# Loads of queries, keys and values moved from just ahead of TensorE's block entries to just behind them

## The chip, the cores and the metric

The kernel runs on one core of one Trainium2 chip. The metric is the device time of one execution in microseconds (us). The kernel before took 391.43 us, the median of three runs (388.89, 391.43 and 392.71 us).

## What is computed

The reference is a retention layer (causal attention with a decay per head in place of a softmax) followed by a mixture of eight experts of which each token uses at most one.

```python
# q, k, v: 8 batches x 8 heads x 576 positions x 64
scores = q @ k.T / sqrt(64)
gamma  = 1 - 2 ** (-5 - head)
x      = (scores * where(i >= j, gamma ** (i - j), 0)) @ v      # as 4608 tokens x 512
# experts: w_gate 512x8, w1 8x512x1024, w2 8x1024x512
for tokens with x @ w_skip > 0:
    e   = argmax(x @ w_gate)
    out = x + softmax(x @ w_gate)[e] * (relu(x @ w1[e]) @ w2[e])
for all others: out = x
```

## The kernel before, in words

**Two stages.** The first stage, to about 148 us, makes the retention output in 36 tiles (`NT`) of 128 rows; nine tiles (`NQ`) cover two batches. The second stage runs the experts over gathered tokens. The change is in the first stage.

**A tile's data.** `u_t[g]` holds the queries and keys of tile g in its first half (s = 0) and the values and the keys in a second layout in its second half (s = 2). Each half is one transfer of 512 KB that SP issues in `load_half` (L513, the transfer L517); the second half of every ninth tile has 256 KB. There are five buffers (`UBUFS`), so a first half can be written only when TensorE has read tile g - 5 for the last time.

**The loop (L857 on).** Step g runs, on TensorE, `scores(g + 1)` (`psc`, `psq`) mixed with `second(g - 1)` (`pxt<-sq,u`), now and then `logits` (`pl`, `pn`), then `state(g)` (`ps_s<-u,kn`) mixed with `values(g - 1)` (`pxt<-u,vs`), then transposes of a finished tile (`px`), and then some of the routing of tokens to experts (`routing`, all on `ps_m`). `in_turn` (L673) mixes two lists of products. GpSimd (POOL) makes `kn` from the second half (`keys(g + 2)`, L602) and `vs` (`rows_of(g + 1)`, L624).

**What sets the order.** TensorE's order is the program's own (a manual schedule). The other queues, SP's among them, are ordered by a scheduler that works from dependences and its own estimate of when an instruction is ready. Second halves are asked for behind the scores of a step, with a wait on TensorE's last product there (L867); first halves at the end of a step, with no wait of their own but that for the buffer (L887); tile 7's first half alone is asked for with the second half (L865, `GLATE = 4`).

**What else SP issues there.** From the time that the first expert is chosen (`choose_first` writes `lead_id`, and SP reads it into a register, L370), SP also loads that expert's weights, 512 KB per transfer (`load_w`, L161), one per step from `weights` (L764).

**The end of the stage.** POOL asks for the first expert's tokens (`xg<-out,gi`, L352) behind the `vs` of the last tiles in its queue, and TensorE turns them (`pt_early`, L741).

A product of plain 32-bit floats is two pairs of instructions on TensorE (a weight load and a matmul each), any other product one pair.

Of the kernel before, what the change touches and what calls it, by code (L numbers as in the profile page):

```python
# [11 lines left out]
F32 = mybir.dt.float32  # L12
# [12 lines left out]
NT = NTOK // P  # L25
# [23 lines left out]
UAHEAD = UBUFS - LAG  # L49
VBUFS = 3  # L50
AHEAD = 5
LEAD = 3
GLATE = 4
GROUPS = (8, 8, 8, 4, 4, 4)
KONE = 2
QD = 32
# [32 lines left out]
def kernel(  # L89
# [9 lines left out]
    nc = tc.nc  # L99
# [15 lines left out]
    def keep_up(n):  # L115
        for _ in range(n):
            nc.tensor.matmul(ps_m, warm[:, :P], warm, start=True, stop=True)
# [375 lines left out]
    with ExitStack() as actx:  # L493
# [19 lines left out]
        def load_half(g, s, after=None):  # L513
            if s == 0:
                u_t[g] = ap.tile([P, 4, NPR, P], F32, tag="u", name=f"u_{g}", bufs=UBUFS)
            n = 1 if s and g % NQ == HALF else 2
            half = nc.sync.dma_start(  # L517
                u_t[g][:, s : s + n].rearrange("p s a i -> p (s a i)"),
                qkv[g, s // 2, :, : n * DM],
            )  # L520
            if after is not None:
                tc.add_manual_dep(
                    half.ins,
                    after.name,
                    mybir.DependencyInfo(mybir.DependencyClass.Sync, mybir.DependencyReason.DATA),
                    reason="the second half begins behind a block of products",
                )

        def last_product():
            return next(i for i in reversed(nc.cur_bb.bb.instructions) if i.engine == mybir.EngineType.PE)  # L530

        nc.scalar.dma_start(tab_sb, tab)
        for g, s in ((0, 0), (1, 0), (0, 2), (2, 0), (1, 2), (3, 0), (2, 2), (3, 2)):
            load_half(g, s)
# [13 lines left out]
        def table(n):  # L548
            times(dq_sb[:, n], mt_sb.unsqueeze(1).broadcast_to([P, NPR, D]), TQ + n, D)
# [11 lines left out]
        def scores(g):  # L561

            u = u_t[g]
            psc_t[g] = [
                pp.tile([P, NPR, P], F32, tag=f"sc{g % 2}", name=f"psc_{g}"),
                pp.tile([P, NPR, D], F32, tag="sc2", name=f"psq_{g}"),
            ]
            for a in range(NPR):
                for c in range(2):
                    q = first(g) if c == 0 else slice(D, P)  # L570
                    for j in range(2):
                        nc.tensor.matmul(  # L572
                            psc_t[g][c][halves[1 - j ^ c], a, : q.stop - q.start],
                            u[halves[j], 1 - j, a, c * D : (c + 1) * D],
                            u[halves[j], j, a, q],
                            start=a == 0,
                            stop=a == NPR - 1,
                            skip_group_check=True,
                        )
                yield  # L580

        def decay(g):

            q = first(g)
            near, far = psc_t.pop(g)
            sc_t[g] = ap.tile([P, NPR, D], F32, tag="sq", name=f"sq_{g}", bufs=2 + LAG)
            nc.vector.tensor_tensor(sc_t[g], far, dq_sb[:, g % NQ // 2], ALU.mult)
            for j in range(2):
                h = halves[1 - j]
                nc.vector.tensor_tensor(  # L590
                    u_t[g][h, j, :, :D], near[h, :, :D], mt_sb[h].unsqueeze(1).broadcast_to([D, NPR, D]), ALU.mult
                )
                if q.stop > D:
                    nc.scalar.copy(u_t[g][h, j, :, D:], near[h, :, D:])  # L594

        def keys(g):
            i = g % NQ
            if i == HALF:
                return
            kn_t[g] = ap.tile([P, NPR, P], F32, tag="kn", name=f"kn_{g}")  # L600
            k = TK + i // 2 * 2
            nc.gpsimd.tensor_tensor(  # L602
                kn_t[g].rearrange("p a (j i) -> p a j i", j=2),
                u_t[g][:, 3].rearrange("p a (j i) -> p a j i", j=2),
                tt_sb[:, k : k + 2, :].rearrange("p j a -> p a j").unsqueeze(3).broadcast_to([P, NPR, 2, D]),
                ALU.mult,
            )
# [10 lines left out]
        def rows_of(g):  # L618

            if 1 < g and g % NQ < 2:  # L620
                clear(g)
            for j in range(2):
                h = halves[1 - j]
                nc.gpsimd.tensor_tensor(  # L624
                    vs_t[g][h, j],
                    u_t[g][h, 2, :, j * D : (j + 1) * D],
                    tt_sb[h, TV + g % NQ // 2, :].unsqueeze(2).broadcast_to([D, NPR, D]),
                    ALU.mult,
                )
# [25 lines left out]
        def second(g):  # L655

            last = g % NQ == HALF
            px_t[g] = pp.tile([P, NPR, P], F32, tag="xt", name=f"pxt_{g}", bufs=2)
            for a in range(NPR):
                for n in range(1 + last):  # L660
                    for j in range(2):
                        h = halves[j]
                        nc.tensor.matmul(  # L663
                            px_t[g][h, a, D:],
                            st_t[g][h, a, :] if n else u_t[g][h, 2, a, j * D : (j + 1) * D],
                            u_t[g][h, j, a, D:] if n else sc_t[g][h, a, :],
                            start=a == 0 and n == 0,
                            stop=False,
                            skip_group_check=True,
                        )  # L670
                yield

        def in_turn(*products):  # L673

            products = list(products)
            while products:
                products = [p for p in products if next(p, p) is not p]

        xt_t = {}

# [20 lines left out]
        def stage_c(g, tag="xn"):  # L701
            b, o = divmod(g, NB)
            px = pp.tile([P, DM], F32, tag=tag, name=f"px_{g}")
            for c in range(NCC):
                nc.tensor.transpose(px[:, c * P : (c + 1) * P], xt_t[b][:, c, o * P : (o + 1) * P], ident)
            xn = ap.tile([P, DM], F32, tag="xn", name=f"xn_{g}")
            nc.scalar.copy(xn.rearrange("t (p c) -> t p c", c=NCC), px.rearrange("t (c p) -> t p c", c=NCC))
            nc.scalar.dma_start(out[g * P : (g + 1) * P, :], xn)
# [92 lines left out]
        def routing(most):  # L801

            for do in added:
                do()
            added.clear()
            for n in range(most):
                if not todo or len(added) == NR or todo[0][1] > g or (n and todo[0][0]):
                    break
                todo.pop(0)[2]()
# [34 lines left out]

        table(0)
        in_turn(scores(0))
        keep_up(NKEEP[0])
        decay(0)
# [8 lines left out]
        for g in range(NT):  # L857
            ahead = g + 1 < NT
            last = g - LAG
            products = [scores(g + 1)] if ahead else []  # L860
            if last >= 0 and last % NQ < HALF:
                products.append(second(last))
            in_turn(*products)
            if g == GLATE:
                load_half(g + UAHEAD - 1, 0, last_product())  # L865
            if g and g + UAHEAD - 1 < NT:
                load_half(g + UAHEAD - 1, 2, last_product())  # L867
            if last >= 0 and last % NQ == HALF:
                in_turn(second(last))
            if ahead:  # L870
                decay(g + 1)
            if g == 0:
                rows_of(1)
            if g + 2 < NT:
                keys(g + 2)
            if g and ahead:
                rows_of(g + 1)
            if g + 1 < len(NKEEP):
                keep_up(NKEEP[g + 1])
            if g < NQ - 1 and g % 2 == 0:  # L880
                table(g // 2 + 1)
            elif g < NQ - 1:
                growth(g // 2 + 1)
            logits(g)
            in_turn(state(g), *([values(last)] if last >= 0 else []))
            if g + 1 != GLATE and g + UAHEAD < NT:
                load_half(g + UAHEAD, 0)  # L887
            if last >= 1:
                stage_c(last - 1)
            routing(0 if g == NT - 1 else 3 if g < starts[KCUT + 1] else 8)  # L890
            weights()
        g = NT
# [521 lines left out]
```

## Time and profile before

| | |
|---|---|
| median of three runs | 391.43 us |
| the profiled execution | 390.34 us |
| its span | 388.6 us |
| TensorE busy | 367.6 us (95%) in 4886 matmuls |
| weight loads of TensorE | 334.5 us (86%) in 4886 |
| VectorE, ScalarE, GpSimd busy | 276.0, 181.7, 152.5 us |
| granted TensorE clock, mean | 0.995 |
| moved by DMA | 106.15 MB, mean 273 GB/s |

The profiled execution is one execution; its time lies 1.09 us below the median of the three runs, and its span leaves out 1.7 us at its ends. Busy times of different engines overlap. The DMA share is the mean busy share of the core's 16 DMA engines.

### The profile page before, as it was taken

The numbers are of one execution on the slowest core, as the hardware profiler recorded it, in microseconds if no ns is written. First come the engines' busy times: TensorE is split into PE (matmuls) and PEld (weight loads), VectorE is DVE, ScalarE is ACT, GpSimd is POOL, SyncE is SP. The second block draws the span as 40 slices with busy tenths as digits, with TensorE's granted clock in tenths as the row PEclk, the third lists the DMA queues.
The fourth block names the chain that finished last, engine by engine and source line by source line (L and its number), as shares of the span: only waits on it lengthen the run. The fifth ranks groups of instructions, "written<-read, shape, count | busy, mean of one in ns | idle before, by whom it ended". The sixth has DMA issues, their size and how long they took to land. (4 is left out here: it accounts for less than half of the span.)

```text
span 388.6 us, 12328 instructions
## 1 busy us (share of the span) xinstructions
PE 367.6 (95%) x4886; PEld 334.5 (86%) x4886; DVE 276.0 (71%) x615; ACT 181.7 (47%) x369; POOL 152.5 (39%) x211
## 2 busy tenths in 40 slices
PE   7899998989999898999999999999999999999991
PEld 3678877777887776888899999999999999999991
DVE  3576677578579794877856767867878768687762
ACT  2464555355544576117445455445545545555311
POOL 5885855555475389260136000420322322002032
PEclk9999999999999999999999999999999999999997
DMA  8989997989999988257899768978899898776511
GB/s 305 404 281 375 394 351 270 347 299 341 320 359 331 313 319 260 63 128 252 261 317 262 264 212 276 327 228 303 275 278 329 249 336 313 233 253 228 142 68 61
DMA packets 49573, 106.15 MB, mean 273 GB/s; under 512 B 6102, under 2 KB 21206, under 8 KB 49511
## 3 DMA queue, kind: packets, MB, share of 16 engines
q1 hardware_dynamic: 40951, 85.81, 65.2%
q0 software_dynamic: 3232, 9.99, 7.9%
q10 hardware_dynamic: 5328, 9.52, 6.5%
q8 instruction: 40, 0.66, 0.7%
q14 instruction: 22, 0.18, 0.1%
HBM read 83.51 MB, written 22.28 MB: 272 GB/s over the span
## 5 line engine op out<-in xcount | busy, mean ns | idle before, releaser
L171 DVE TENSOR_TENSOR wlo_w<-w,whi_w 128x1024 fp32r<-128x1024 f32 x59 | 72.0, 1223 | 37.8 <-ACT whi_w L170 35.4
L170 ACT CAST whi_w<-w 128x1024 fp32r<-128x1024 f32 x59 | 61.7, 1050 | 33.1 <-PE py L465 32.4
L465 PE MATMUL py<-hlo,whi_w 128*128 128x336 f32 (+6 forms) x224 | 67.8, 303 | 0.0
L465 PE MATMUL ph<-xhi,wlo_w 128*128 128x336 f32 (+6 forms) x224 | 67.6, 302 | 0.0
L465 PE MATMUL ph<-xlo,whi_w 128*128 128x336 f32 (+6 forms) x224 | 67.5, 302 | 0.0
L465 PE MATMUL ph<-xhi,whi_w 128*128 128x336 f32 (+6 forms) x224 | 67.5, 301 | 0.0
L465 PE MATMUL py<-hhi,wlo_w 128*128 128x336 f32 (+6 forms) x224 | 67.5, 301 | 0.0
L465 PE MATMUL py<-hhi,whi_w 128*128 128x336 f32 (+6 forms) x224 | 67.4, 301 | 0.0
L1035 POOL DMA_INDIRECT out<-rs,sidx x17 | 21.2, 1245 | 84.0 <-DVE rs L1034 82.8
L624 POOL TENSOR_TENSOR vs<-u,tab_sb 64x256 f32<-64x256 f32 x72 | 46.7, 649 | 9.9 <-DMA u<-qkv 2.7
L602 POOL TENSOR_TENSOR kn<-u,tab_sb 128x512 f32<-128x512 f32 x32 | 33.8, 1057 | 42.5 <-DMA u<-qkv 18.9
L687 PE MATMUL pxt<-u,vs 128*64 128x128 f32 (+1 forms) x576 | 47.8, 269 | 1.6 <-issue 1.6
L473 ACT ACTIVATE hhi<-ph 128x336 fp32r<-128x336 f32 (+8 forms) x61 | 25.8, 423 | 45.3 <-PE ph L465 45.0
L590 DVE TENSOR_TENSOR u<-psc,tab_sb 64x256 f32<-64x256 f32 x72 | 30.3, 420 | 23.4 <-PE pxt L663 7.7
L594 ACT COPY u<-psc 64x256 f32<-64x256 f32 x64 | 23.4, 366 | 48.7 <-DVE u L590 45.6
L465 PEld LDWEIGHTS ph<-xhi,whi_w 128*128 128x128 f32 x224 | 42.3, 189 | 0.1
L465 PEld LDWEIGHTS py<-hlo,whi_w 128*128 128x128 f32 x224 | 42.2, 188 | 0.2 <-DVE hlo L474 0.2
L465 PEld LDWEIGHTS ph<-xlo,whi_w 128*128 128x128 f32 x224 | 42.3, 189 | 0.1
L465 PEld LDWEIGHTS py<-hhi,whi_w 128*128 128x128 f32 x224 | 42.3, 189 | 0.0
L465 PEld LDWEIGHTS ph<-xhi,wlo_w 128*128 128x128 f32 x224 | 42.3, 189 | 0.0
L465 PEld LDWEIGHTS py<-hhi,wlo_w 128*128 128x128 f32 x224 | 42.3, 189 | 0.0
L572 PE MATMUL psc<-u 64*64 64x128 f32 (+1 forms) x576 | 39.1, 272 | 2.3 <-DMA u<-qkv 2.1
(213 smaller groups left out, 780.7 us busy)
## 6 DMA issues: line engine op xcount, KB each, us to landing
u<-qkv SPq DMA_DIRECT2D x68, 512.0 KB, 6.6
w<-w SPq DMA_DIRECT2D x64, 512.0 KB, 5.5
out<-xn ACTq DMA_DIRECT2D x36, 256.0 KB, 5.8
hop<-xg SPq DMA_DIRECT2D x12, 256.0 KB, 5.2
xh<-hop SPq DMA_DIRECT2D x48, 64.0 KB, 4.9
hopy<-yp SPq DMA_DIRECT2D x24, 128.0 KB, 3.4
yr<-hopy SPq DMA_DIRECT2D x6, 512.0 KB
u<-qkv SPq DMA_DIRECT2D x4, 256.0 KB
```

The costliest lines, as they stand in the source:

```text
L170: nc.scalar.copy(hi, t)
L171: nc.vector.tensor_tensor(lo, t, hi.bitcast(F32), ALU.subtract)
L465: nc.tensor.matmul(ps, x, y, start=first and n == 0, stop=last and n == 3 * len(terms) - 1)
L473: nc.scalar.activation(hi, ph, AF.Relu)
L572: nc.tensor.matmul(psc_t[g][c][halves[1 - j ^ c], a, : q.stop - q.start], u[halves[j], 1 - j, a, c * D : (c + 1) * D], u[halves[j], j, a, ...
L590: nc.vector.tensor_tensor(u_t[g][h, j, :, :D], near[h, :, :D], mt_sb[h].unsqueeze(1).broadcast_to([D, NPR, D]), ALU.mult)
L594: nc.scalar.copy(u_t[g][h, j, :, D:], near[h, :, D:])
L602: nc.gpsimd.tensor_tensor(kn_t[g].rearrange("p a (j i) -> p a j i", j=2), u_t[g][:, 3].rearrange("p a (j i) -> p a j i", j=2), tt_sb[:, k ...
L624: nc.gpsimd.tensor_tensor(vs_t[g][h, j], u_t[g][h, 2, :, j * D : (j + 1) * D], tt_sb[h, TV + g % NQ // 2, :].unsqueeze(2).broadcast_to([D, ...
L687: nc.tensor.matmul(pxt[halves[j], a, q], vs_t[g][:, j, a, :], u_t[g][:, j, a, q], start=False, stop=a == NPR - 1, skip_group_check=True,)
L1035: done = nc.gpsimd.indirect_dma_start(out=out, out_offset=bass.IndirectOffsetOnAxis(ap=idx, axis=0), in_=rs[:n], in_offset=None, bounds_ch ...
```

## The change

A function `words` counts the instructions that TensorE has been given so far: four for a product of 32-bit floats, two for any other or a transpose, and one more for every 95. The program takes an entry to a block of 256 to lie where this count is 193 modulo 256. `load_clear` asks, for each half, how far the next entry is: if it is at most 93 words away for a first half, or 68 for a second one, the load is put off until 32 words behind that entry, with a wait on the product that stands there; a load that comes up while another is put off follows it. `load_put_off` issues what is due, and is called in the middle of mixed products as well. The rule holds from step 3 on (`GLATE = 3`); the special case for tile 7 goes away. By the program's own count 14 first halves are put off, by 8 to 121 words (1012 in all), and 9 second halves, by 16 to 135 words (689 in all), ahead of 17 different entries; tile 7's first half is issued 49 words earlier than before.

```diff
--- before.py
+++ after.py
@@ -50,7 +50,12 @@
 VBUFS = 3
 AHEAD = 5
 LEAD = 3
-GLATE = 4
+GLATE = 3
+BLOCK = 256
+ENTRY = 193
+WAITED = 95
+SOON = (93, 68)
+BEHIND = 32
 GROUPS = (8, 8, 8, 4, 4, 4)
 KONE = 2
 QD = 32
@@ -529,6 +534,33 @@
         def last_product():
             return next(i for i in reversed(nc.cur_bb.bb.instructions) if i.engine == mybir.EngineType.PE)
 
+        seen = [0, 0]
+
+        def words():
+
+            traced = nc.cur_bb.bb.instructions
+            for i in traced[seen[0] :]:
+                if i.engine == mybir.EngineType.PE:
+                    seen[1] += 2 if i.is_transpose or i.ins[0].dtype != F32 else 4
+            seen[0] = len(traced)
+            return seen[1] + seen[1] // WAITED
+
+        put_off = []
+
+        def load_clear(t, s):
+
+            n = words()
+            entry = n + (ENTRY - n) % BLOCK
+            soon = g >= GLATE and entry - n <= SOON[s // 2]
+            if put_off or soon:
+                put_off.append((entry + BEHIND if soon else put_off[-1][0], t, s))
+            else:
+                load_half(t, s, last_product() if s else None)
+
+        def load_put_off():
+            while put_off and words() >= put_off[0][0]:
+                load_half(*put_off.pop(0)[1:], last_product())
+
         nc.scalar.dma_start(tab_sb, tab)
         for g, s in ((0, 0), (1, 0), (0, 2), (2, 0), (1, 2), (3, 0), (2, 2), (3, 2)):
             load_half(g, s)
@@ -675,6 +707,7 @@
             products = list(products)
             while products:
                 products = [p for p in products if next(p, p) is not p]
+                load_put_off()
 
         xt_t = {}
 
@@ -861,10 +894,8 @@
             if last >= 0 and last % NQ < HALF:
                 products.append(second(last))
             in_turn(*products)
-            if g == GLATE:
-                load_half(g + UAHEAD - 1, 0, last_product())
             if g and g + UAHEAD - 1 < NT:
-                load_half(g + UAHEAD - 1, 2, last_product())
+                load_clear(g + UAHEAD - 1, 2)
             if last >= 0 and last % NQ == HALF:
                 in_turn(second(last))
             if ahead:
@@ -883,10 +914,11 @@
                 growth(g // 2 + 1)
             logits(g)
             in_turn(state(g), *([values(last)] if last >= 0 else []))
-            if g + 1 != GLATE and g + UAHEAD < NT:
-                load_half(g + UAHEAD, 0)
+            if g + UAHEAD < NT:
+                load_clear(g + UAHEAD, 0)
             if last >= 1:
                 stage_c(last - 1)
+            load_put_off()
             routing(0 if g == NT - 1 else 3 if g < starts[KCUT + 1] else 8)
             weights()
         g = NT
```

No instruction is added on any engine, and the orders of TensorE, VectorE, ScalarE and GpSimd are those of before. SP's queue and its waits change. The first place is SP's queue around tiles 20 to 22 (`u_20` to `u_22`; each tile's first row is its first half, and `PE` in a wait is a product of TensorE). Before:

```order
L517 DMA u_19_1366<-qkv 128x1024 [waits DMAHW1_49,PE_49,DMAHW6_49,Activation_49,Pool_49]
L517 DMA u_19_1366<-qkv 128x1024 [waits DMAHW0_49,PE_49]
L517 DMA u_20_1440<-qkv 128x1024 [waits DMAHW1_49,PE_49,DMAHW4_49,Activation_49,Pool_49]
L517 DMA u_20_1440<-qkv 128x1024 [waits DMAHW3_49,PE_49]
L517 DMA u_21_1508<-qkv 128x1024 [waits DMAHW4_49,PE_49,DMAHW7_49,Activation_49,Pool_49]
L517 DMA u_21_1508<-qkv 128x1024 [waits DMAHW6_49,PE_49]
L517 DMA u_22_1607<-qkv 128x1024 [waits DMAHW2_49,DVE_49,DMAHW7_49,PE_49,Pool_49]
```

With the change:

```order
L522 DMA u_19_1366<-qkv 128x1024 [waits DMAHW0_49,PE_49,DMAHW6_49,Activation_49,Pool_49]
L522 DMA u_19_1366<-qkv 128x1024 [waits DMAHW0_49,PE_49]
L522 DMA u_20_1457<-qkv 128x1024 [waits DMAHW2_49,Activation_49,Pool_49]
L522 DMA u_20_1457<-qkv 128x1024 [waits DMAHW3_49,PE_49]
L522 DMA u_21_1547<-qkv 128x1024 [waits DMAHW5_49,PE_49,DMAHW7_49,Activation_49,Pool_49]
L522 DMA u_21_1547<-qkv 128x1024 [waits DMAHW6_49]
L522 DMA u_22_1607<-qkv 128x1024 [waits DMAHW0_49,DVE_49,DMAHW1_49,PE_49,Pool_49]
```

The first half of tile 20 has lost its wait on TensorE, since it now stands behind the put-off second half of tile 19, whose product is the later one; the second half of tile 21 has lost its own in the same way, behind the put-off first half of that tile.

The second place is SP's queue where the first expert's weights come in (`w_0_0` to `w_0_2`) among the last tiles' halves (`u_33` to `u_35`); `DMAHW3` and the like are the counters on which a transfer's landing is told. Before:

```order
L161 ISA
L161 DMA w_0_0_2522<-w 128x1024 [waits DMAHW2_49]
L517 DMA u_33_2489<-qkv 128x1024 [waits DMAHW3_49,PE_49]
L517 DMA u_34_2602<-qkv 128x1024 [waits DMAHW4_49,PE_49,DMAHW6_49,Activation_49,Pool_49]
L161 ISA
L161 DMA w_0_1_2633<-w 128x1024 [waits DMAHW6_49]
L517 DMA u_34_2602<-qkv 128x1024 [waits DMAHW7_49,PE_49]
L517 DMA u_35_2693<-qkv 128x1024 [waits DMAHW0_49,PE_49,DMAHW1_49,Activation_49,Pool_49]
L161 ISA
L161 DMA w_0_2_2719<-w 128x1024 [waits DMAHW2_49]
L517 DMA u_35_2693<-qkv 128x512 [waits DMAHW3_49,PE_49]
```

With the change:

```order
L166 ISA
L166 DMA w_0_0_2522<-w 128x1024 [waits DMAHW2_49]
L166 ISA
L166 DMA w_0_1_2630<-w 128x1024 [waits DMAHW3_49]
L166 ISA
L166 DMA w_0_2_2717<-w 128x1024 [waits DMAHW4_49]
L522 DMA u_33_2489<-qkv 128x1024 [waits DMAHW6_49,PE_49]
L522 DMA u_34_2642<-qkv 128x1024 [waits DMAHW7_49,Activation_49,Pool_49]
L522 DMA u_34_2642<-qkv 128x1024 [waits DMAHW0_49,PE_49]
L522 DMA u_35_2734<-qkv 128x1024 [waits DMAHW1_49,PE_49,DMAHW2_49,Activation_49,Pool_49]
L522 DMA u_35_2734<-qkv 128x512 [waits DMAHW3_49,PE_49]
```

The second half of tile 33 stood behind one transfer of weights and now stands behind three; the first half of tile 34 stood behind one (with tile 33's half) and now stands behind three as well; tile 35's first half stands behind three and not two, its second half behind the same three as before.

## Rows read from the trace of the kernel before

**Rows 1.** The page, busy us of each engine, share of the span, instructions:

```profile
PE 367.6 (95%) x4886; PEld 334.5 (86%) x4886; DVE 276.0 (71%) x615; ACT 181.7 (47%) x369; POOL 152.5 (39%) x211
```

**Rows 2.** TensorE's waits in 0 to 156 us: us, times, longest:

```profile
PE psc L572 <- DMA u<-qkv: 2.1, 3, 1.2
PE pt_early L741 <- DMA xg<-out,gi: 1.8, 1, 1.8
PE pxt L687 <- issue: 1.6, 2, 1.4
```

**Rows 3.** Timeline of TensorE: start, us, what, [idle before it <- releaser], five places:

```profile
36.93 0.32 PE L572 MATMUL psc<-u 64*64 64x128 f32 x1 [0.25 <-issue]
...
52.81 0.32 PE L687 MATMUL pxt<-u,vs 128*64 128x128 f32 x1 [0.29 <-issue]
...
75.94 0.27 PE L663 MATMUL pxt<-u,sv 64*64 64x64 f32 x1 [0.77 <-issue]
...
82.37 0.33 PE L687 MATMUL pxt<-u,vs 128*64 128x128 f32 x2 [1.35 <-issue]
...
118.56 0.27 PE L572 MATMUL psq<-u 64*64 64x64 f32 x1 [0.45 <-issue]
```

**Rows 4.** Stretches between those places: us, busy (xinstructions) by engine, clock, DMA share:

```profile
52.82:75.95 23.13, 21.08 (x508) 17.11 (x509) 15.88 (x44) 11.15 (x27) 12.42 (x19) 1.00 0.90 311
75.95:82.37 6.42, 5.07 (x127) 4.34 (x127) 5.11 (x16) 2.51 (x7) 3.55 (x6) 1.00 0.97 357
82.37:118.56 36.19, 35.30 (x887) 29.72 (x888) 26.13 (x72) 19.08 (x47) 20.71 (x31) 1.00 0.92 329
```

**Rows 5.** The page, DMA queues: packets, MB, share of 16 engines:

```profile
q8 instruction: 40, 0.66, 0.7%
```

**Rows 6.** Timeline of SP's queue, two loads ahead of the idle at 75.94:

```profile
68.41 0.33 SPq L517 DMA_DIRECT2D u<-qkv  x1
...
70.00 0.33 SPq L517 DMA_DIRECT2D u<-qkv  x1
```

**Rows 7.** The page, DMA issues: KB each, median us from issue to landing:

```profile
u<-qkv SPq DMA_DIRECT2D x68, 512.0 KB, 6.6
```

**Rows 8.** Stretches of the stage, columns as in Rows 4; the last is GB/s:

```profile
24.00:120.00 96.00, 91.17 (x2224) 74.51 (x2226) 68.26 (x182) 48.43 (x119) 58.14 (x85) 1.00 0.93 336
120.00:131.00 11.00, 11.00 (x281) 9.72 (x281) 10.42 (x35) 5.40 (x15) 5.45 (x8) 1.00 0.88 277
131.00:143.00 12.00, 9.81 (x232) 8.16 (x230) 9.59 (x33) 8.27 (x16) 8.00 (x12) 1.00 1.00 391
```

**Rows 9.** Timeline of SP's queue: first weights, tile 33's second half, tile 35's:

```profile
124.95 0.36 SPq L161 DMA_DIRECT2D w<-w  x1
...
125.41 1.29 SPq L517 DMA_DIRECT2D u<-qkv  x1
...
133.61 0.33 SPq L517 DMA_DIRECT2D u<-qkv  x1
```

**Rows 10.** SP's waits in 119 to 135 us: us, times, longest:

```profile
SPq L517 <- DMA u<-qkv: 3.2, 1, 3.2
...
SPq L370 <- DVE u L590: 2.6, 1, 2.6
```

**Rows 11.** Timeline of TensorE: scores of tiles 34 and 35, first gathered tokens:

```profile
134.86 0.33 PE L572 MATMUL psc<-u 64*64 64x128 f32 x2 [1.21 <-DMA u<-qkv]
...
140.00 0.28 PE L572 MATMUL psc<-u 64*64 64x64 f32 x2 [0.60 <-DMA u<-qkv]
...
150.37 1.10 PE L741 MATMUL pt_early<-ident,xg 128*128 128x128 f32 x7 [1.80 <-DMA xg<-out,gi]
```

**Rows 12.** Timeline of POOL, the end of the first stage:

```profile
133.71 1.06 POOL L602 TENSOR_TENSOR kn<-u,tab_sb 128x512 f32<-128x512 f32 x1 [6.04 <-PE ps_m L232]
...
142.21 1.29 POOL L624 TENSOR_TENSOR vs<-u,tab_sb 64x256 f32<-64x256 f32 x2 [0.91 <-DMA u<-qkv]
143.68 1.22 POOL L352 DMA_INDIRECT xg<-out,gi  x1 [0.17 <-POOL vs L624]
```

## The prediction, made before the change was run

> **What bounds the kernel now.** I read the page's busy times first. TensorE is busy 367.6 us of a span of 388.6 us [rows 1], so it bounds the kernel, and a change to loads is worth what it does to TensorE's idle times in the stage that uses them. So next its list of waits from 0 to 156 us. Three entries bear on this change: idle that the profile cannot explain ("issue") ahead of `pxt`, 1.6 us in two places; idle until loads of `u` land, 2.1 us in three places; and 1.8 us until the first gathered tokens land [rows 2].
>
> Then the timeline, for where the unexplained idle lies. There are five such places in the stage that go with the change's count: 0.25, 0.29, 0.77, 1.35 and 0.45 us, together 3.1 us [rows 3]. The reader is to see that different products stand there, so it isn't one kind of work that waits. The stretches between them show what they share: from 75.95 to 82.37 us TensorE runs 127 matmuls and 127 weight loads, 254 instructions; from 52.82 us it is 1017, from 82.37 us 1775 [rows 4]. These are 1, 4 and 7 times 256, less some 1% that waits or missing records can make up. So these idle times lie on the grid of 256 on which the change's rule is built. The page has a DMA queue of kind "instruction" with 40 packets, 0.66 MB [rows 5]; TensorE's 2 x 4886 instructions [rows 1] make 38 blocks of 256. I take it that each packet brings one block of TensorE's program, and that in the five places the block came late. The trace's views don't show when a packet was asked for or moved; this is inferred.
>
> The DMA view of the stage completes it: the 16 engines are busy 93% from 24 to 120 us and 100% from 131 to 143 us, at 391 GB/s [rows 8]. Both TensorE and the DMA engines are near full, so late instruction packets are plausible, and a load that is put off has little idle DMA time to be made up in.
>
> **The change, part by part.** *The entries.* The change moves 23 halves from ahead of 17 entries to behind them. Counting in the program's order, each of the five late blocks follows one block after an entry of those 17: for the idle at 75.94 us these are the loads issued at 68.41 and 70.00 us [rows 6], just ahead of and about at the entry one block earlier. If a late packet is one that queued behind loads, all five go. Bounds: at most 3.1 us [rows 3] is won; at least nothing, and a loss is possible through the queue (a rival below). I take 2.8 us: the two long ones and all but one of the three short ones, whose mean is 0.33 us, because the loads do not vanish but come about 0.6 us behind the entry (32 instructions; 256 take 5.07 us of TensorE's busy time [rows 4], 0.020 us each) and now and then in pairs.
>
> *The delay of the halves.* 1701 instructions over 23 halves is a mean of 74, or 1.5 us; the longest is 135, or 2.7 us. A load lands 6.6 us (median) after its issue [rows 7], while 512 KB at 391 GB/s is 1.34 us [rows 8]: most of the 6.6 us is spent behind earlier loads. A later issue shortens that waiting instead of delaying the landing, as long as the queue doesn't run dry, so I cost these delays at nothing. The cover is those earlier loads. If it is gone, scores wait by up to the delay: they waited for `u` in only three places [rows 2]. Tile 7's earlier first half (49 instructions, 1.0 us) is worth nothing either.
>
> *SP's queue at the first expert's weights.* Here the order of transfers changes, which costs more than a shift. SP waits 2.6 us for the choice of the expert [rows 10] and issues the first weights at 124.95 us [rows 9]. Before, tile 33's second half follows at once, then tile 34's first; now the weights `w_0_1` and `w_0_2` go in front of both. Landings of before: SP's wait at 133.61 us [rows 9, 10] is on the counter that tile 33's second half shares with tile 35's, so that half landed at 133.6 us; tile 34's first half landed at 134.86 us, tile 35's first at 140.00 us [rows 11], its second, of 256 KB, at 142.21 us, where POOL waits for it [rows 12]. From 133.6 to 142.2 us this is five and a half transfers of 512 KB: 1.56 us each. Two in front cost 3.1 us (bounds: 2 x 1.34 = 2.7 us at 391 GB/s; 3.4 us by the three transfers from 134.86 to 140.00 us). TensorE would have the scores of tile 34 at about 138.0 us.
>
> What reaches the end is set by POOL. Its `kn` at 133.71 us is put down to a product, but its data landed at 133.6 us too; moved to 136.7 us, it drags the work behind it, `vs`, and then the request for the first expert's tokens (143.68 us), less the 0.91 us that POOL now idles for tile 35's second half, whose landing doesn't move [rows 12]. So the request comes 3.0 - 0.9 = 2.1 us later, and the tokens for which TensorE idles at 150.37 us [rows 11] as well. TensorE's own delay (3.1 us, less the 0.60 us it waits for tile 35) disappears in that idle. Bounds 1.7 and 2.5 us. This is a loss of 2.1 us.
>
> *Passing it on.* The shift of 2.8 us gained earlier has to get through the DMA engines. From 24 to 120 us they idle 7% of 96 us, 6.7 us, and from 120 to 131 us 12%, 1.3 us [rows 8]. That is enough, so I count the whole gain.
>
> *Sum.* 2.1 - 2.8 = -0.7 us. On the profiled execution that gives 390.34 - 0.7 = 389.6 us. The median of before lies 1.09 us above it, so against the median I expect 391.43 - 0.7 = **390.7 us**. About 1% (3.9 us) is what a measurement of this kernel can tell from no change: below 387.5 is faster, above 395.3 slower.
>
> **The rivals.** *First: a block's packet doesn't wait for the loads issued ahead.* With DMA engines busy 90 to 97% between the idle places [rows 4], there are always loads queued, wherever one puts them. Then only the weights' order is left: 391.43 + 2.1 = 393.5 us. For it: 17 entries have a load ahead, and only five late blocks follow; four more entries of that stretch have none. If lateness fell on entries at random, all five would be among the 17 of 21 with a chance of about a third, so the five agreeing is weak evidence. Against it: the two longest follow the entries with two put-off halves each. The Trainium skill's page "DMA: Bandwidth & Descriptors", in "Queues, rings and completion order", says that each DMA engine takes turns between its queues, one packet of one queue at a time; by that rule a fetch waits for the packet in service and not for all that was issued earlier, and this rival's 393.5 us would be the time. No view here shows a fetch's wait, so the trace neither confirms nor excludes it.
>
> The skill's page "Runtime: NRT & Kernel Launch", in "Instruction fetch mechanics", says that crossing a boundary of 256 instructions is mostly hidden; by that rule too the entries would be worth nothing. The 1.35 and 0.77 us idles exactly one block apart [rows 3, 4] speak against it here.
>
> *Second: the weights cost nothing and all five idles go.* TensorE already idles 1.8 us at the tokens [rows 11], and POOL's request may have been waiting for its list and not for `vs`: POOL idles 0.17 us ahead of it [rows 12], so the slack is small. Then 391.43 - 3.1 = 388.3 us.
>
> *Third, slower: the load queue runs dry.* A put-off load leaves the DMA engines idle, and what they lose they can't make up. They have 6.7 us idle from 24 to 120 us [rows 8]; at more than 6.7 / 23 = 0.29 us of new idle per put-off half they, and not TensorE, set the stage's length. At 0.5 us each (a third of the mean delay) the stage takes 89.3 us of transfers and 11.5 us of idle, 100.8 us in place of 96: 391.43 + 4.8 = 396.2 us. For it: the queue is at 85 to 100%, and the halves often go in pairs. Against it: 6.6 us to landing [rows 7] is four times a transfer.
>
> **How the numbers follow.** Chances: the forecast 0.45, the first rival 0.23, the second 0.19, the third 0.13. The forecast's own bounds: 3.1 won and 1.7 lost gives 390.0 us; nothing won and 2.5 lost gives 393.9 us, at the first rival. Medians of three runs of before spread over 3.8 us, so each case has about 1 us on either side. The range is 387.3 to 394.9 us: it takes in the first two rivals with their spread, and leaves out the third and some of the second. Faster by over 1% needs more than all the idle at entries: only the second rival's lower tail, 0.07. Slower by over 1% is the third rival: 0.13. Within 1%: 0.80.
>
> **What the profile of the changed kernel would show.** Right: no unexplained idle of over 0.4 us on the grid of 256; TensorE's wait for `u` at tile 34 up from 1.21 to 3 us or more; SP issuing three transfers of weights in a row near 125 us; the request for tokens 2 us later than it would be by TensorE's progress. First rival: idle of the same sum at other entries. Second: the request for tokens moves with TensorE. Third: more and longer waits of `psc` for `u` before tile 30, and a DMA share from 24 to 120 us below 0.90. I would be wrong altogether if the scores' waits for `u` grew to over 5 us while the weights' order cost nothing.

## The result, and the profile after

The change made the kernel slower by about 1%: 392.67 us, the median of 21 executions (390.16 to 396.59 us), against 390.87 us for the kernel before in 21 executions on the same chip (385.65 to 394.68 us). The ratio is **1.0095, with a 95% interval of 1.0067 to 1.0123**: 3.7 us more, where 0.7 us less was forecast. Ratios here and below leave disturbed executions out, which is why they need not be the ratio of the two medians. The profiled execution took 394.84 us.

The page's busy times and the granted clock in 40 slices of the span (tenths of full speed):

```profile
PE 370.8 (94%) x4886; PEld 335.9 (85%) x4886; DVE 278.7 (71%) x615; ACT 181.6 (46%) x369; POOL 152.5 (39%) x211
PEclk9999999999999989999999999999999999999998
```

The same 4886 matmuls are busy 3.2 us longer than before [rows 1], and one slice in the middle, the fifteenth, shows an 8. The second points to TensorE's clock; the first alone would not, since e1 below is busy 370.0 us with no such slice. Next TensorE's waits from 0 to 160 us (us, times, longest):

```profile
PE psc L604 <- DMA u<-qkv: 5.0, 5, 3.3
PE psq L604 <- issue: 3.6, 3, 1.7
...
PE px L738 <- DVE xt L732: 1.2, 1, 1.2
...
PE pxt L720 <- issue: 0.9, 3, 0.4
...
PE pt_early L774 <- DMA xg<-out,gi: 0.2, 1, 0.2
```

Against before [rows 2]: waits for `u` rose from 2.1 to 5.0 us, unexplained idle ahead of `psq` and `pxt` from 2.9 us in four places [rows 3] to 4.5 us in six, and the wait at the first tokens all but went. The timeline places them (start, us, what, [idle before it <- releaser]):

```profile
33.12 0.65 PE L738 MATMUL px<-ident,xt 128*128 128x128 f32 x4 [1.19 <-DVE xt L732]
...
45.17 0.33 PE L604 MATMUL psc<-u 64*64 64x128 f32 x2 [0.81 <-DMA u<-qkv]
...
51.50 0.27 PE L604 MATMUL psq<-u 64*64 64x64 f32 x2 [1.70 <-issue]
...
63.62 0.27 PE L604 MATMUL psq<-u 64*64 64x64 f32 x1 [1.08 <-issue]
...
84.09 0.33 PE L720 MATMUL pxt<-u,vs 128*64 128x128 f32 x2 [0.44 <-issue]
...
122.68 0.27 PE L604 MATMUL psq<-u 64*64 64x64 f32 x1 [0.86 <-issue]
...
141.02 0.33 PE L604 MATMUL psc<-u 64*64 64x128 f32 x2 [3.30 <-DMA u<-qkv]
```

And the stretches between three of them (matmuls and weight loads in brackets behind PE's and PEld's busy times):

```profile
51.51:63.63 12.12, 10.86 (x255) 8.78 (x254) 9.56 (x29) 5.95 (x15) 5.44 (x8) 1.00 0.80 265
63.63:84.10 20.47, 20.03 (x510) 16.90 (x510) 13.64 (x32) 9.56 (x24) 12.33 (x19) 1.00 0.95 339
```

509 and 1020 instructions are two and four times 256, less some records: the late blocks are on the same grid as before [rows 3, 4], but at other entries, and no smaller. At 33.12 us the releaser named, `xt`, is only the nearest event; the idle stands on the grid too.

The end of the stage is where the forecast's second term lay. SP's queue, then POOL, then stretches of TensorE (busy by engine, clock, DMA share, GB/s):

```profile
125.76 0.33 SPq L522 DMA_DIRECT2D u<-qkv  x1
128.26 2.29 SPq L166 DMA_DIRECT2D w<-w  x3
130.81 4.75 SPq L522 DMA_DIRECT2D u<-qkv  x5
```

```profile
139.85 1.06 POOL L634 TENSOR_TENSOR kn<-u,tab_sb 128x512 f32<-128x512 f32 x1 [8.12 <-DMA u<-qkv]
...
149.75 1.22 POOL L357 DMA_INDIRECT xg<-out,gi  x1 [0.96 <-POOL vs L656]
```

```profile
120.00:131.00 11.00, 9.76 (x245) 7.83 (x246) 9.95 (x35) 5.99 (x16) 6.54 (x9) 1.00 0.97 343
131.00:141.50 10.50, 6.80 (x182) 6.06 (x175) 7.11 (x25) 4.96 (x11) 2.23 (x4) 1.00 0.98 369
131.00:145.00 14.00, 10.30 (x222) 7.78 (x213) 9.47 (x32) 5.82 (x13) 5.65 (x10) 0.88 0.93 354
141.50:145.50 4.00, 4.00 (x66) 2.22 (x60) 2.55 (x7) 1.24 (x3) 3.92 (x7) 0.57 0.69 271
```

Three weights go in a row, the scores of tile 34 then wait 3.30 us for their half, as forecast. New is the last stretch: behind that idle the granted clock falls to 0.57 on the mean of 4 us, which is mostly the 1.2 GHz level, and TensorE does 66 matmuls there with no idle. From the same clock rows, a mean of 0.88 over 14 us is 14 x 2 x 0.12 = 3.4 us at half clock, a loss of 1.7 us. Before, the clock was 1.00 from 24 to 143 us [rows 8]. This is one profile; what the other executions say stands with x9 and x10.

### The profile page after: what moved, and what is told of

The parts are those of the page before. It is cut to its first block, busy times and chain, and to the rows that moved or that the text cites. A ratio compares the mean times of both kernels' runs of the same rounds, so it can differ in the third digit from the quotient of the medians.

```text
span 393.1 us, 12293 instructions
## 1 busy us (share of the span) xinstructions
PE 370.8 (94%) x4886; PEld 335.9 (85%) x4886; DVE 278.7 (71%) x615; ACT 181.6 (46%) x369; POOL 152.5 (39%) x211
## 5 line engine op out<-in xcount | busy, mean ns | idle before, releaser
L604 PE MATMUL psc<-u 64*64 64x128 f32 (+1 forms) x576 | 40.3, 274 | 5.1 <-DMA u<-qkv 5.0
```

The costliest lines, as they stand in the source:

```text
L604: nc.tensor.matmul(psc_t[g][c][halves[1 - j ^ c], a, : q.stop - q.start], u[halves[j], 1 - j, a, c * D : (c + 1) * D], u[halves[j], j, a, ...
```

## The experiments

Three theories were set against each other. **W**: the order of the weights costs, through POOL's request for tokens. **C**: it costs through the clock that falls behind the long idle. **B**: the halves put off go in bunches and make later blocks late, so the early part costs by itself. In the diffs a minus is a line of the change, or of the kernel before where that is said.

**e1_early and e2_late: half of the change each.** e1 puts off halves up to step 29 alone (all but those around the weights), e2 from step 30 on alone.

```diff
-            soon = g >= GLATE and entry - n <= SOON[s // 2]
+            soon = GLATE <= g < 30 and entry - n <= SOON[s // 2]   # e1_early
-GLATE = 3
+GLATE = 30                                                         # e2_late
```

> The put-off rule holds only up to step 29, so the order of the first expert's weights among the last tiles' halves is that of the kernel before; the 20 put-off halves of tiles 7 to 32 stay put off. Theory W (the weights in front of tile 33's half are the loss): 0 to 2 us faster than before, since only the entries are left. Theory B (put-off halves come in bunches, a bunch makes the next blocks of TensorE's program late and leaves the load queue dry ahead of it): 1.5 to 3 us slower than before, unexplained idle on the grid of 256 of 3 us or more, as with the whole change.

> The put-off rule holds only from step 30 on: three halves (tiles 33, 34, 35) are put off and two transfers of weights stand in front of them, everything earlier is as before but for tile 7's first half. Theory W: 2 us slower than before (1.7 to 2.5), scores of tile 34 waiting 3 us or more for their data. Theory B: the weights' order costs under 1 us, because TensorE's delay disappears in its wait for the first tokens.

Measured: e1 1.0052 (1.0015 to 1.0089), e2 1.0142 (1.0075 to 1.0209). The late part looks the dearer one, though the intervals touch, e2 has only six executions, and the two parts add up to more than the whole change's 1.0095. e1 was 2.0 us slower, as B had it, with 2.1 us of idle on the grid where B wanted 3; its repeat, below, was not slower. In e2 the wait at tile 34 and the clock:

```profile
137.15 0.48 PE L604 MATMUL psc<-u 64*64 64x128 f32 x2 [3.53 <-DMA u<-qkv]
```

```profile
131.00:145.00 14.00, 10.14 (x194) 7.88 (x194) 7.30 (x27) 6.49 (x14) 8.46 (x12) 0.76 0.85 329
```

A mean of 0.76 is 6.7 us at half clock.

**e3_entry65: the same rule half a block off the grid.**

```diff
-ENTRY = 193
+ENTRY = 65
```

> The same rule with the entry taken to lie half a block (128 instructions) away, so that halves are put off from the middle of a block to 96 instructions ahead of the real entry; the order of the weights is nearly that of before. If what counts is how near ahead of an entry a load is issued: more unexplained idle than before and than with the change, 3 us or more slower than before. Theory B (bunches as such): about as slow as the early half of the change alone, 1.5 to 3 us. If the place on the grid and the bunches count for nothing: as before within 1 us.

Measured: 1.0271 (1.0221 to 1.0321). TensorE's waits show more unexplained idle than any other kernel here:

```profile
PE pxt L720 <- issue: 3.6, 3, 1.6
...
PE psq L604 <- issue: 1.4, 1, 1.4
PE pl L746 <- issue: 1.1, 1, 1.1
```

Its span is 6.1 us longer than that of before (394.7 against 388.6 us), and 4.5 us of this are idle on the grid (7.6 against 3.1 us). So where the loads lie against the grid does matter here, although `ENTRY` also decides which halves are put off and for how long, and the end of the stage isn't as before either: tile 35's second half goes behind four transfers of weights, and POOL waits 2.57 us for it at 148.90 us. That is not yet a gain for the right half.

**after_again: the change once more,** for a second profile.

> The changed kernel once more, beside the others on the same chip, for a second profile. Both theories: 2 to 4 us slower than before. The places of the unexplained idle need not be those of the first profile; theory B wants their sum at 3 us or more again, theory W at less than before's 3.1 us.

Measured: 1.0092 (1.0057 to 1.0127). The wait at tile 34 is 2.90 us and the clock from 131 to 145 us is 0.88 again; the late blocks on the grid sum to 1.1 us here and to 5.7 us in the first profile. One profile's late blocks are not the kernel's.

**x5_busy: TensorE kept busy through the wait,** by eleven extra products into the bank of tile 34's scores, which the scores then overwrite.

```diff
+            for _ in range(11 if g == 34 else 0):
+                nc.tensor.matmul(psc_t[g][0]..., ident, gt_sb[:, 0]..., start=True, stop=True, ...)
```

> The whole change, with 11 extra products (128x512, some 0.27 us each, 2.9 us in all) put ahead of the scores of tile 34, into the bank that these scores then overwrite, so that TensorE works while tile 34's first half is awaited. Theory C (the 3 us of idle at tile 34 let the granted clock fall to half for 3 to 7 us behind it, and that is most of what the weights' order costs): granted clock 1.00 from 131 to 145 us, 1.5 to 2.5 us faster than the change, 1.003 to 1.006 of before. Theory W (the loss is POOL's late request for the tokens, 2.1 us, and the clock matters little): no faster than the change, 1.009 of before.

Measured: 1.0198 (1.0152 to 1.0245). The clock stayed at 1.00, but the timeline shows that the products were mis-sized:

```profile
132.54 9.69 PE L601 MATMUL psc<-gt_sb,ident 128*128 128x512 f32 x22
```

9.69 us is some 6 us more than the wait: each of the 22 passes took 0.44 us, and each product is two of them. So the time says nothing about the clock's price. The expectation of the time was a miss; x9 and x10 repeat it with three products.

**x6_light: less to load** (in the kernel before, second halves from tile 5 on are cut to 256 KB, and the values stand in for the keys' second layout, so the tokens go to other experts and only the first stage may be read).

```diff
-            n = 1 if s and g % NQ == HALF else 2
+            n = 1 if s and (g % NQ == HALF or g > 4) else 2
```

> The kernel before with the second halves of tiles 5 to 35 cut to the values (256 KB in place of 512 KB); the keys of their second layout are left out and the values used in their place, so its output is not the reference's and only the stage to 145 us is to be read. If late blocks of TensorE's program come from the load on the DMA engines: under 0.5 us of unexplained idle on the grid of 256 from 24 to 120 us, where the kernel before has 3.1. If the blocks are late for another reason: 2 us or more, as before.

Measured: the DMA engines' share from 24 to 120 us fell from 0.93 to 0.85, yet blocks came late at 32.19 us (0.64 us), 37.28 (0.25), 91.19 (1.02), 117.16 (0.85) and 135.48 us (2.20). From 24 to 120 us that is 2.8 us, the "2 us or more" of the expectation. Relieving the engines by a twelfth doesn't remove late blocks. That they wait for loads at all is not shown by this run.

**x7_entry125: the loads a quarter of a block earlier,** with e1's bound at step 29.

```diff
-ENTRY = 193
+ENTRY = 125
```

> The put-off rule with the entry taken to lie 68 instructions (1.4 us) earlier, up to step 29 only: halves that would be issued 68 to 161 instructions ahead of a real entry are put off until 36 ahead of it. If the loads that count are those whose data are queued by the time of the entry, about 1 to 1.5 us after their issue, this is the window to clear: less idle at entries than with the change's own window, 1 us or more faster than the early half of the change, at or below before. Theory B (a bunch behind the window is what costs): as the early half of the change, 1.003 to 1.008 of before. If the worst place for a bunch is just ahead of an entry: between that and the 1.027 of the half-block shift.

Measured: 1.0015 (0.9985 to 1.0044), no worse than e1 with the rule's own place. The idle at entries was not less but 6.1 us in its profile, the most but e3's, and yet its span was 387.8 us, 0.8 us under that of before: its waits for `u` up to 148 us sum to 0.4 us (1.8 before), and it has no wait at the first tokens (1.8 before). So idle at entries doesn't lengthen the kernel one for one.

**x8_wlast: the kernel before, with the weights' order turned the other way:** `w_0_1` to `w_0_3` are issued behind tile 35's halves. Minus is the kernel before.

```diff
-            if n < AHEAD:
+            if n in (0, 4):
                 chunks[n] = load_w(0, n, regs)
+            elif n == 3:
+                with tc.issue_after(halves_in[0].ins):
+                    for m in (1, 2, 3):
+                        chunks[m] = load_w(0, m, regs)
```

> The kernel before with no load put off, but the weights w_0_1 and w_0_2 issued behind tile 35's halves: the reverse of what the change does to that order. Theories W and C: tile 34's second half and tile 35's halves land 1.5 to 3 us sooner, TensorE's wait at tile 35 (0.60 us) and POOL's (0.91 us) go, the clock falls no more often than before: 0.5 to 2 us faster than before. If these weights are needed as early as they came: slower, TensorE waiting for the first expert's split weights.

Measured: 0.9998 (0.9969 to 1.0028). The 0.5 to 2 us that W and C expected did not come. TensorE's waits for `u` did go, but this profile has 5.8 us of late blocks. So no gain is shown from taking the one weight ahead of tile 34's half out of the way, and no cost from loading the weights later, within 1.2 us.

**x11_put_wlast: the whole change, with x8's order of the weights.**

> The change with all its halves put off, but w_0_1, w_0_2 and w_0_3 issued behind tile 35's halves. Weights' order as the dear half of the change: wait at tile 34 under 1.5 us, clock of 131 to 145 us 1.00, ratio as the kernel with the early halves put off, 1.002 to 1.006. Rival B (late halves themselves, put off, are what costs): wait at tile 34 still 3 us, ratio 1.008 to 1.010.

Measured: **0.9993 (0.9962 to 1.0024)**. This one edit takes back the 1%. Wait at tile 34, and the stretch:

```profile
134.14 0.33 PE L605 MATMUL psc<-u 64*64 64x128 f32 x2 [0.22 <-DMA u<-qkv]
```

```profile
131.00:145.00 14.00, 12.12 (x270) 9.73 (x266) 10.34 (x38) 9.19 (x19) 10.71 (x14) 1.00 0.94 347
```

**x9_after3 and x10_late3: the clock's share.** Three of x5's products (`range(3 ...)`), in the change and in e2.

> The change, with three extra 128x512 products (out of ident and the gate's table, into the bank of tile 34's scores, which overwrite it) ahead of tile 34's scores, so that TensorE is busy instead of idle for most of its 3.3 us wait; the 22 passes of the earlier run with eleven took 9.69 us, so three take about 2.6. Theory C (the wait itself is nearly paid for at the tokens, what costs is the half clock behind it): clock of 131 to 145 us 1.00, idle left at tile 34 under 1 us, time about 3 us under the change, ratio to before 1.001 to 1.004. Rival W (the wait delays POOL's kn and its request for tokens, the clock matters little): ratio as the change's, 1.008 to 1.010.

> The same three products in the kernel that puts off tiles 33 to 35 alone (measured 1.0142 without them). Theory C: clock of 131 to 145 us 1.00 where it was 0.76, ratio 1.000 to 1.006. Rival W: 1.012 to 1.016.

Measured: x9 1.0049 (1.0015 to 1.0084), x10 1.0053 (1.0025 to 1.0081). The timeline and the stretch of x9:

```profile
135.51 2.82 PE L601 MATMUL psc<-gt_sb,ident 128*128 128x512 f32 x6
138.26 0.33 PE L613 MATMUL psc<-u 64*64 64x128 f32 x2
```

```profile
131.00:145.00 14.00, 13.60 (x279) 10.12 (x279) 10.42 (x34) 8.72 (x19) 7.76 (x11) 1.00 0.93 357
```

The order of the transfers is still the change's, but TensorE isn't idle ahead of tile 34's scores and the clock stays at 1.00. 2.8 us of useless work make the kernel 0.9954 and 0.9912 times as long (1.0049 / 1.0095, 1.0053 / 1.0142): 1.8 and 3.5 us, against 1.7 and 3.4 us worked out from the half clock in the two profiles. The intervals within each pair overlap a little, so these sizes are rough. The granted clock of every execution agrees: its mean is 0.993 and 0.991 in the two sets of the change (29 executions), 0.987 in e2 (6), and 0.994 to 0.996 in x9, x10, x11 and the kernel before. The differences, times 390 us, are 0.7 to 1.6 us for the change, where the clock fell in some executions and not in others, and 3.0 us for e2. Theory C holds for that part. What is left, 0.5% or 2.0 us in both, fits theory W: the halves still go behind three weights, and POOL's `kn` waits for its data.

```profile
136.85 1.06 POOL L643 TENSOR_TENSOR kn<-u,tab_sb 128x512 f32<-128x512 f32 x1 [7.19 <-DMA u<-qkv]
...
146.02 1.23 POOL L357 DMA_INDIRECT xg<-out,gi  x1 [0.17 <-POOL vs L665]
```

The request comes 2.3 us later than before [rows 12], but the first weights were issued 1.9 us later too (124.95 us before [rows 9]), which is not the order's doing. SP's issues of x9, then SP and POOL of x11:

```profile
126.82 2.24 SPq L166 DMA_DIRECT2D w<-w  x3
```

```profile
125.22 0.35 SPq L166 DMA_DIRECT2D w<-w  x1
...
142.51 1.23 POOL L357 DMA_INDIRECT xg<-out,gi  x1 [0.96 <-POOL vs L657]
```

From the issue of the first weights to the request it is 17.3 us in x11 and 19.2 us in x9. The other profiles fall into the same groups: 16.3 to 18.7 us, 17.5 on the mean, in the nine with fewer than three weights in front of tile 33's half (before, e1, e1_again, x7, x8, x11, x12, x12_again, x13); 19.2 and 19.6 us with them in front and the clock kept up (x9, x10); 20.4, 21.2 and 21.5 us where the clock fell (after_again, e2, after). Left out are x5 and x6, and e3 with its own order (19.9 us). That is 1.9 us for the order and 1.6 us for what hangs on the clock. Some tenths of the 2.0 us left may be the extra products' own, since TensorE goes from them to the scores with no idle left.

**x12_behind8, x12_again, e1_again and x13_both: does the delay cost?** x12 is e1 with `BEHIND = 8` in place of 32, so that halves come some 24 words sooner, 0.5 us at 0.020 us each (the "2.6 us" of the expectation is wrong); e1 and x12 were repeated; x13 is x11 with `BEHIND = 8` (its delay is not "a quarter": the mean of 74 words falls by about a third).

```diff
-BEHIND = 32
+BEHIND = 8
```

> Halves put off up to step 29 only, but issued 8 instructions behind the entry in place of 32, some 2.6 us sooner. If the early halves cost through their delay (tile 11's scores waited 0.8 to 1.05 us): that wait falls under 0.3 us and the ratio to 0.999 to 1.003. Rival B (what costs is that the blocks of the next entries come late all the same): tile 11's wait may go, the idle on the grid of 256 stays at 2 us or more, ratio 1.004 to 1.007.

> The early halves put off by 8 in place of 32, once more (0.9975 before). Theory D: under the kernel with 32 by 0.003 or more, at 0.996 to 0.999. Theory N: within 0.002 of it, 0.998 to 1.002.

> The early halves alone put off, 32 behind, once more (1.0052 before; with the late halves and the weights last 0.9993). If putting off early halves by 32 costs by itself (theory D, by the waits of scores for the halves that come late): ratio 1.003 to 1.007. If it is worth nothing either way (theory N: late blocks only change places): 0.998 to 1.002.

> All halves put off as in the change, by 8 in place of 32, and w_0_1, w_0_2, w_0_3 behind tile 35's halves: no half is behind a weight and the delay is a quarter. Theory D: 0.996 to 0.999, no wait over 0.5 us at the scores of tiles 11 and 34. Theory N: 0.998 to 1.002. If late halves cost beside the weights: over 1.003.

Measured: x12 0.9975 (0.9947 to 1.0004) and again 0.9968 (0.9931 to 1.0004); e1 again 1.0008 (0.9978 to 1.0038); x13 0.9988 (0.9953 to 1.0022). With 32 words behind, two kernels without the weights' trouble gave 1.0052 and 1.0008 (e1) and 0.9993 (x11); with 8 words, 0.9975, 0.9968 and 0.9988. The order is the one that a cost of the delay would give, about 0.4%, but the intervals of e1_again and x11 overlap all three of the short delay, and TensorE's waits for `u` up to 130 us speak against it (2.0 and 1.8 us in the two profiles of x12, 0.3 us in e1_again's): open. No version is shown to be faster than the kernel before, since no interval lies wholly under 1; the three with the short delay, each at 0.5 to 1.2 us under it, may be.

**Late blocks over all profiles.** I summed idle of 0.15 us or more ahead of instructions of TensorE within a few of a multiple of 256 (counted in the timeline), from 20 to 145 us, one profile of each kernel:

| loads of the early steps | sums, us | mean |
|---|---|---|
| as before: before, e2, x8, x10 | 3.1, 2.3, 5.8, 3.5 | 3.7 |
| put off behind 193: after, after_again, e1, e1_again, x5, x9, x11, x12, x12_again, x13 | 5.7, 1.1, 2.1, 2.2, 1.1, 2.6, 2.8, 1.3, 1.7, 1.9 | 2.3 |
| put off behind 125 or 65: x7, e3 | 6.1, 7.6 | 6.9 |

Put off, the late blocks are fewer by 1.4 us on the mean, half of what was forecast, with groups that overlap and four profiles in the smaller one.

**When a block's packet moves.** The prediction says that the views don't show it. The DMA view of a narrow window does, since it lists the instruction queue's packets. In the kernel before, from 79.70 to 79.80 us (packets, MB, share of 16 engines):

```profile
q8 instruction: 1, 0.02, 60.6%
```

The share is that of 16 engines over 0.1 us, so this packet took 0.97 us. In all five places of [rows 3] a packet took 0.9 to 1.0 us and ended 1.3 to 1.6 us ahead of the late product, and it had started 2.5 to 4.4 us behind the entry one block earlier. There is one such packet to a block. I counted the entries from 20 to 130 us in the 16 profiles of the table by the loads that SP had issued in the 1.9 us (93 words) ahead of the entry one block earlier:

| loads ahead | entries | packet's start behind that entry, mean us | late blocks |
|---|---|---|---|
| none | 112 | 2.2 | 8 |
| one | 171 | 2.6 | 44 |
| two or more | 39 | 3.3 | 17 |

So in these profiles a block's packet does come later behind such loads, as the prediction took it; this compares places, and is not an edit of its own. But the put-offs clear only half of the entries: with the loads put off behind 193, 104 of 201 entries still have a load ahead, against 75 of 82 with the loads as before.

## Why the prediction was wrong

**The entries: the step that failed.** It read that the five late blocks of one profile each follow loads just ahead, had "all five go" and took 2.8 us as won. The tie to the loads holds (the count of packets above), but the saving doesn't. Late blocks change from one execution of the same kernel to the next (1.1 and 5.7 us with the change), so five places of one profile were not five causes, and half of the entries keep a load ahead of them. On the mean perhaps 1.4 us go, and the time shows none of it: 1.0052, 1.0008 and 0.9993 where nothing but the put-offs is left. Nor was "the whole gain" passed on, as x7 shows from the other side. The first rival, which gave the entries nothing, was right about their worth in time, but its reason, that a packet doesn't wait for the loads issued ahead, goes against the count. The Trainium skill's page "DMA: Bandwidth & Descriptors", in "Queues, rings and completion order", has each engine take turns between queues by the packet; by that rule the grid would not matter, and the count, and e3's 1.0271 with nothing but `ENTRY` changed, differ. Where a packet spends the time before it starts is not shown by any run here.

**The delay "costed at nothing": the second step that failed.** New waits of scores for halves put off exist: 0.81 us at 45.17 us (tile 11, whose first half is put off 121 words) and 1.05 us in after_again; e1 has 0.97 us there, which its profile puts down to ACT's `xn`; in e1_again and x11 tile 11 doesn't wait. Up to 130 us, waits for `u` sum to 0.3 us before and to nothing in e2, x8 and x10, whose early loads are as before; in the ten profiles with put-offs behind 193 they sum to 0.2 (x9) to 2.1 us (after_again), 1.2 us on the mean. Against some 1.4 us of late blocks saved that makes a sum near nothing. It is argued from the rows, not shown: the two profiles of x12 have 2.0 and 1.8 us of these waits, and x12 isn't slower.

**The weights' order: right in the wait, too small by half in the cost.** "Two in front cost 3.1 us", a wait of "3 us or more" at tile 34, three weights in a row: measured 3.30, 2.90 and 3.53 us, and three in a row. The cost was put at 2.1 us through POOL's request. Measured against x11 it is 1.0095 - 0.9993, 1.0% or 4.0 us, give or take 1.6 us by the two intervals: about 2.0 us as forecast (x9, x10), and about 2 us that the sum did not have, because it let TensorE's own delay "disappear" in the idle at the tokens. The delay did disappear there (0.2 us left at `pt_early`, 1.80 before). But behind the idle the clock fell, to the 1.2 GHz level for 3.4 us in both profiles of the change and 6.7 us in e2. By the granted clock of all executions this took 0.7 to 1.6 us in the change, so the clock may not be all of these 2 us. The rule stands in the Trainium skill, page "TensorE: Matmul & The Clock Gate", "Why this matters for your kernels": to avoid drops in mid-kernel it asks for no long idle gaps between bursts of matmuls, as the clock goes back to half. The trace agrees, with the rows above; the prediction had the gap and did not ask what the clock would do.

**The sum.** Forecast 2.1 - 2.8 = -0.7 us. Measured: 4.0 (the weights' order, nearly half of it with the clock) - 0.3 (all put-offs, x11, not different from 0) = 3.7 us. Of the 4.4 us between the two, 2.5 us are the entries' missing gain and 1.9 us the weights' order. The range took in the measured time only because it was wide: the forecast was for a little less, and the time rose.

**The other signs.** "No unexplained idle of over 0.4 us on the grid": wrong, five places in the first profile. "The request for tokens 2 us later": 2.3 us in x9; in the change's own profile 6.07 us [rows 12], of which 3.3 us were there when the first weights were issued (128.26 against 124.95 us [rows 9]). The third rival's mechanism, DMA engines that run dry, is not what happened: their share from 24 to 120 us is 0.91 and 0.93 in the two profiles of the change, and in x11, which is no slower, 0.94; waits for `u` up to 130 us sum to 1.7 us in the change's first profile, against 0.3 before.

## What to carry to other kernels

Before pricing an idle that a later wait will absorb, ask how long TensorE stands still in one piece: two waits of 1 us and one of 3.3 us are not worth the same, since the clock may fall behind the long one, and useless products put into it can pay. Transfers that go in front of others in a full queue are to be counted one by one, and what cured it here was to order them by when they are needed (x11). Idle that lies on the grid of the program's blocks should be read from several profiles before a change is built on it.

## What the runs showed that was not expected

The clock fell behind shorter idles too. In x12_again it fell behind one of 1.9 us, at 125 us (waits, then stretches):

```profile
PE pn L761 <- ACT xn L740: 1.9, 1, 1.9
```

```profile
118.00:125.00 7.00, 5.24 (x141) 3.92 (x136) 6.56 (x24) 3.55 (x8) 3.56 (x5) 1.00 0.95 355
125.00:129.00 4.00, 3.90 (x39) 3.40 (x40) 2.91 (x12) 1.42 (x6) 1.67 (x3) 0.60 0.84 292
```

A mean of 0.60 over 4 us is 3.2 us at half clock. In x6 it fell behind the idle of 2.20 us at 135.48 us:

```profile
136.00:145.00 9.00, 8.81 (x153) 7.07 (x147) 6.38 (x22) 5.55 (x12) 4.36 (x6) 0.81 0.56 196
```

An idle of 1.80 us in the kernel before [rows 11] and one of 1.70 us in the change left the clock alone. So a late block of TensorE's program can cost more than its idle, as in x6, where one came 2.20 us late. The Trainium skill's page "Runtime: NRT & Kernel Launch", in "Instruction fetch mechanics", calls the cost of a block boundary mostly hidden; these profiles show 1.1 to 7.6 us of idle at boundaries per execution in this stage.
